# Filter groups in twos, rows of the last groups from two queues, and a projection moved ahead: a four-layer kernel on one core

## Chip, cores and metric

One core of a Trainium2 chip runs the whole kernel. Its engines are TensorE (PE, with its weight loads as PEld), VectorE (DVE), ScalarE (ACT), GpSimd (POOL) and SyncE (SP); each runs its own instructions in the order in which they were written. The metric is the device time of one execution in microseconds (us), lower is better.

## What is computed

The input x has 2048 rows and 576 columns, in float32. Two layers are applied in turn, each twice (`_layernorm` has no weights):

```python
def _A_ref(x, wqkv, wo):          # H = 32 heads of 18, window W = 256
    q, k, v = split((x @ wqkv))
    scores = einsum("bhqd,bhkd->bhqk", q, k) * Dh ** -0.5
    scores = where((i - j >= 0) & (i - j < W), scores, -1e9)
    return (softmax(scores) @ v) @ wo

def _B_ref(x, w_r, w_i):
    X = rfft2(x) * (w_r + 1j * w_i)
    return irfft2(X, s=(S, D))

x = x + _A_ref(_layernorm(x), A_wqkv, A_wo)
x = x + _B_ref(_layernorm(x), B_w_r, B_w_i)
x = x + _A_ref(_layernorm(x), A_wqkv, A_wo)
x = x + _B_ref(_layernorm(x), B_w_r, B_w_i)
```

## The kernel before

The 2048 rows are 16 tiles of 128 (NT = 16). The program runs `layer_a`, `layer_b`, `layer_a`, `layer_b`, each overlapping its neighbours at the borders. Everything is written out by hand: an instruction stands in its engine's queue where the Python code emits it. `pipe(n, [(lag, fn), ...])` calls, at step s, each `fn` for tile s − lag, in the order of the list. A DMA is issued by the engine whose queue it is written in; those of SP and ScalarE share eight semaphore lanes in rotation, and one waits until the last transfer on its lane has landed. DMAs of GpSimd have lanes of their own.

**layer_a.** `first_tiles` writes the beginning of the first one by hand, before the steps of a loop with lags go on: `ld` loads a tile, `sq`, `bn`, `bn2` make mean and variance, `f0` normalises (`axn`), `f1` transposes it on PE (`tpaa`, `tpba`) and splits it in high and low parts `xh`, `xl` on ScalarE and VectorE, `f2` multiplies by the weights of v (`vps`) and copies the result (`vt`) for a store to `v_d`. Then `proj` makes q and k by quarters of 512 rows: PE `pj`, ScalarE copies to `sg`, VectorE the remainder, a DMA stores it to `qk_d`, from where it is loaded into `qs` and `ks`. A tiny activation `ex` (L1045) is written ahead of them so that the table of exponentials is loaded early; its one-element tile comes from the pool `wp` of that stage. `score_max` finds row maxima; `m_rows` (L1134) turns the negated maxima of a quarter (`mt`) into rows of `qs` by four small DMAs (L1144); `exps` makes E on PE and P = exp(E) on ScalarE. For the first two quarters of the first head group the four DMAs are ScalarE's, later SP's.

**layer_b.** The output projection of layer_a (`out.unit`, PE tile `ops`, 28 matmuls for a tile of rows, then two VectorE additions in `late`) is interleaved with the forward transform: in the second layer `norm(u)` is the norm of tile u (`out.stats`, then `fy`), `out.sums` its squares on ScalarE, `back(n)` is `f3` (PE `pz`) and `f4` (copy `half`, sums `ye`, DMA issues). `f4` stores `ye` to DRAM as `yd[0]`, and for tiles from 11 on copies eight rows directly into the tiles of the first two filter groups. In the second layer the stores of tiles 12 and 13 are held until tile 15 and then issued by ScalarE.

The filter stage runs over 16 groups g. `g0` loads y, `gw` the weights, `g1m` makes `p2_g` on PE (eight matmuls of 128 rows into 64 columns; the page's counts of eight include the halves), four products on VectorE (L475, L476 with two tiles each) and `uv` on GpSimd; `g2` makes `pq` on PE (L488), a copy `both` on ScalarE (L510), a difference on GpSimd (L513) and two on VectorE (L514, L515), and stores the result (`ze`, or `eo` for even groups) as `yd[1]`. PSUM comes from `Banks`: tiles with the tag "mm" rotate over three slots.

```python
zs, held = {}, []
pipe(16, [(10, g2), (7, g1m), (2, gw), (0, g0)])
```

The inverse stage follows, `pipe` over the 16 tiles with `ly` (load a tile, L545), `i1` (PE `pi`), `i2` (transposes) and `i3` (PE `po`, and the output). The first `near` tiles (2 in the first layer_b, 3 in the second) aren't loaded by `ly`: `g2` puts them together in SBUF, the groups below FG = 11 by `older` reads from `yd[1]` (L519), the others by `rows`, a DMA of eight rows from SBUF to SBUF (L495):

```python
def rows(eng, n2, k):
    eng.dma_start(yis[n2][8 * k:8 * k + 8]..., zs[k][8 * n2:8 * n2 + 8])
```

The store of group 13 is held and issued after the rows of group 15. Between the stages of the second layer_b `warm(n)` runs n matmuls whose result nobody uses. In the first layer_b five further tiles (`w0`, `w1`, `w2`, PE `wo`) of layer weights run beside the stages; `w1(3)` (transposes, and the ScalarE copy `et19`) follows the copy of group 15.

Of the kernel before, what the change touches and what calls it, by code (L numbers as in the profile page):

```python
# [117 lines left out]
class Banks:  # L118
# [6 lines left out]
    def tile(self, shape, dtype, tag, name, bufs):  # L125
        if tag != "mm":
            return self.pools[tag not in self.lower].tile(shape, dtype, tag=tag, name=name, bufs=bufs)
        self.turn = (self.turn + 1) % 3
        return self.pools[self.turn == 2].tile(shape, dtype, tag=tag, name=name, bufs=2 if self.turn < 2 else 1)

def layer_b(tc, xf, dst, dcs, gc, ident, rh, rl, out, ga_d, fc_d, m2_d, w_d, wo_d, wo2_d, dram, nxt, share):
# [8 lines left out]
    FD, FG, SH = 11, 11, 192  # L140
    near, NY = (2, 3) if first else (3, 4)
    with ExitStack() as stack:
# [152 lines left out]
        def f4(n2, h):  # L295
            pz = h["pz"]
            ye = wp.tile([128, 2, NF], F32, tag="ye", name=f"ye{n2}", bufs=NY)
            if not first and NT - 4 <= n2 < NT - 1:
                if "both" not in h:
                    f4c(n2, h)  # L300
                both = h["both"]
                V.tensor_add(ye[:, 0], pz[:, 0, 0:NF], both[:, 1])
                P.tensor_sub(ye[:, 1], both[:, 0], both[:, 1])
            else:
                both = ip.tile([128, 2, NF], F32, tag="both", name=f"half{n2}", bufs=2)
                A.copy(both[:, 0], pz[:, 1, 0:NF])
# [103 lines left out]
        else:  # L410
# [51 lines left out]
        def g1m(g, h):  # L462
            ps = pp.tile([128, 2, 512], F32, tag="mm", name=f"p2_{g}", bufs=3)
# [17 lines left out]
        def g2(g, h):  # L481
            pq = pp.tile([128, 2, 512], F32, tag="mm", name=f"pq{g}", bufs=3)
# [14 lines left out]
            if g == 15:  # L497
# [3 lines left out]
                if first:  # L501
                    w1(3)
                else:
                    rows(nc.scalar, 2, 13)
                    rows(nc.scalar, 2, 14)
                for n2 in range(near):
                    rows(nc.sync, n2, 15)
                held.pop()()
            else:
                A.copy(both, pq[:, :, 0:NF])  # L510
                if near > 2 and g in (FG + 1, FG + 2):
                    rows(nc.scalar, 2, g - 1)
# [3 lines left out]
            if g in (FG - 1, FG + 1):  # L516
                lo, hi = (0, 8) if g < FG else (8, FG)
                for n2 in range(near):
                    nc.sync.dma_start(yis[n2][8 * lo:8 * hi].rearrange("p c f -> p (c f)"), yd[1][n2, lo:hi].rearrange("g i f -> (g i) f"))  # L519
# [6 lines left out]
            if g == 13:  # L526
                held.append(store)
            else:
                store()
# [135 lines left out]
class Out:  # L665
# [108 lines left out]
    def late(self, u):  # L774
        oL = self.oL[u % 3]
        h, l = oL[:, 0:128], oL[:, 128:256]
        self.steps(u, [(h, "h", 3), (l, "h", 3), (h, "l", 3)], False, True)
        x = self.xt(u)
# [29 lines left out]
    def unit(self, u, pp):  # L808
        ps = pp.tile([128, 2, 512], F32, tag="mm", name=f"ops{u}", bufs=3)
        self.early(u, [ps[:, 0], ps[:, 1]])  # L810
        self.late(u)
# [11 lines left out]
def layer_a(tc, ident, eps, bp, src, dst, wqk_d, wv_d, wo_d, dc_d, gc_d, dram, copy, wvs, second, spectral, share):  # L823
# [17 lines left out]
    if True:  # L841
# [24 lines left out]
        with tc.tile_pool(name="a1", bufs=2) as wp, ExitStack() as banks:  # L866
# [108 lines left out]
            def first_tiles():  # L975
# [32 lines left out]
                f2(0, h[0], slice(1, 14))  # L1008
                f2(1, h[1], slice(0, 8))
# [4 lines left out]
            for s in range(0 if second else 7, NT + 7 + late):  # L1014
# [7 lines left out]
                for lag, fn in ((0, ld), (6 + late, f1), (4, sq), (4 + second, bn2), (4 + 2 * second, f0), (3, bn), (7 + late, f2)):  # L1022
                    if 0 <= s - lag < NT:
# [7 lines left out]
        with ExitStack() as c2:  # L1031
# [13 lines left out]
            A.activation(wp.tile([128, 1], F32, name="ex", bufs=1), eps, AF.Exp)  # L1045
# [88 lines left out]
            def m_rows(n, c):  # L1134
# [5 lines left out]
                for hp in range(2):  # L1140
                    for pair in range(2):
                        r = (hp * 2 + pair) * 4
                        b = 64 * hp + 63
                        (nc.sync if n or c > 1 else nc.scalar).dma_start(q[b:b + 1, pair, c * 512:c * 512 + 512].rearrange("a (t q) -> a t q", t=4).bitcast(F32),  # L1144
# [328 lines left out]
```

## Time and profile before

| | us |
|---|---|
| median of three runs (1383.33, 1384.60, 1388.88) | 1384.6 |
| the profiled execution | 1387.57 |
| its span, first to last instruction | 1385.1 |
| PE busy | 1343.1 (97%) |
| VectorE, ScalarE, GpSimd busy | 893.3, 785.4, 640.0 |
| TensorE clock granted, mean | 0.994 |
| filter stage, first layer_b (p of group 0 to pq of group 15) | 605.1 to 643.4 |
| filter stage, second layer_b | 1269.7 to 1312.1 |

In the rows of the profile an instruction is named by its line in the kernel (L488), engine, operation, and output and input tiles without their numbers (`pq<-uv,m`); "x8" means eight in a row. `ofree` is a large shared buffer in which y, the tiles `yis` and x lie. ACTq, SPq are the DMA issues of an engine's queue, times in us from the start of the span. In brackets stands the idle time ahead of a row and what ended it.

### The profile page before, as it was taken

The page shows a single profiled execution, that of the slowest core. Times are in us where ns is not written, and L with a number is a line of the kernel's source. Part 1 is how long each engine was busy: PE and PEld are TensorE (multiplying, and loading weights), DVE is VectorE, ACT ScalarE, POOL GpSimd, SP SyncE. Part 2 cuts the span into 40 slices and gives each one's busy share as a digit, 9 for nine tenths or more (in the row PEclk, how much of TensorE's full clock was granted, in tenths as well). Part 3 has the DMA queues.
Part 4 walks back from the last instruction along what each step waited for, and adds up shares of the span by engine and source line. Part 5 has one row for each costly group of instructions (what it writes and reads, how often), then busy time and mean ns, then how long its engine had stood idle before and what let it go on. Part 6 is the DMA issues. An engine that isn't in the chain of part 4 may idle for free.

```text
span 1385.1 us, 33553 instructions
## 1 busy us (share of the span) xinstructions
PE 1343.1 (97%) x11356; PEld 1001.1 (72%) x11356; DVE 893.3 (64%) x3046; ACT 785.4 (57%) x1978; POOL 640.0 (46%) x1140
## 2 busy tenths in 40 slices
PE   8999999999999999998999999999999999998988
PEld 8986666666665699975999866666666655897577
DVE  4417777877778266666673157787777883564745
ACT  5522777777778544443355316777777777563223
POOL 2257555555447443475221394554545457102711
PEclk9999999999999999999999999999999999999999
DMA  6756655655446457678763468555555465597864
GB/s 192 211 160 204 190 181 174 189 167 163 145 150 185 109 166 239 218 244 258 254 224 73 107 199 232 169 163 168 165 157 143 151 181 147 171 349 247 257 224 158
DMA packets 202159, 259.09 MB, mean 187 GB/s; under 512 B 104270, under 2 KB 109646, under 8 KB 201478
## 3 DMA queue, kind: packets, MB, share of 16 engines
q1 hardware_dynamic: 191494, 235.63, 55.8%
q10 hardware_dynamic: 8000, 15.63, 3.2%
q0 software_dynamic: 2496, 5.71, 1.5%
q8 instruction: 91, 1.49, 0.4%
q14 instruction: 78, 0.64, 0.2%
HBM read 156.26 MB, written 101.01 MB: 186 GB/s over the span
## 4 chain that ended last, share of the span: by engine, by line
PE 83%; DMA 5%; ACT 3%; DVE 3%; POOL 2%; issue 2%; SPq 1%; ACTq 0%; DVEq 0%; POOLq 0%
PE pj L1067 16%; PE S L1124 12%; PE U L1181 11%; PE vps L963 8%; PE ops L758 7%; PE E L1161 5%; PE po L251 4%; PE pq L488 2%; PE pf L251 2%; PE p L467 2%; PE tpo L1195 2%; PE pi L551 2%; ACT P L1162 2%; PE pz L289 2%; DMA yd<-ze 1%
## 5 line engine op out<-in xcount | busy, mean ns | idle before, releaser
L1126 DVE CUSTOM_DVE_ANT_0 jk<-S,mask 128x384 bf16<-128x384 f32 (+2 forms) x1024 | 490.4, 529 | 109.4 <-PE E L1161 56.1
L1162 ACT ACTIVATE P<-E 128x384 f32<-128x384 f32 (+2 forms) x1024 | 409.0, 476 | 121.9 <-PE E L1161 98.7
L1164 POOL TENSOR_SCALAR_AFFINE_SELECT P<-P 128x512 f32<-128x512 f32 x256 | 163.1, 637 | 277.9 <-ACT P L1162 254.3
L1124 PE MATMUL S<-ks,qs 63*128 63x384 f32 (+2 forms) x1024 | 269.1, 371 | 1.0 <-DVE m L1126 0.4
L1161 PE MATMUL E<-qs,ks 64*128 64x384 f32 (+2 forms) x1024 | 222.2, 372 | 3.3 <-ACT P L1162 2.6
L1124 PEld LDWEIGHTS S<-ks,qs 63*128 63x128 f32 x1024 | 140.7, 185 | 105.2 <-DVE m L1126 73.1
L1181 PE MATMUL U<-P,vq 128*19 128x128 f32 (+1 forms) x3840 | 187.8, 328 | 1.0 <-ACT us L1186 1.0
L1067 PE MATMUL pj<-xh,wqh 128*128 128x512 f32 x360 | 156.4, 434 | 3.3 <-DVE sg L1082 2.8
L1181 PEld LDWEIGHTS U<-P,vq 128*19 128x19 f32 x3840 | 95.7, 98 | 77.5 <-issue 21.7
L1167 POOL TENSOR_SCALAR_AFFINE_SELECT P<-P 128x512 f32<-128x512 f32 x224 | 142.8, 638 | 0.0
L1161 PEld LDWEIGHTS E<-qs,ks 64*128 64x128 f32 x1024 | 114.1, 185 | 17.0 <-ACT P L1162 8.2
L1067 PE MATMUL pj<-xh,wql 128*128 128x512 f32 x360 | 124.5, 419 | 0.5 <-POOL wql L648 0.5
L1067 PE MATMUL pj<-xl,wqh 128*128 128x512 f32 x288 | 122.1, 424 | 0.0
L758 PE MATMUL ops<-oroom 128*128 128x290 f32 (+1 forms) x812 | 116.3, 300 | 0.2
L758 PEld LDWEIGHTS ops<-oroom 128*128 128x128 f32 x812 | 111.4, 191 | 0.7 <-DVE ofree L781 0.7
L1067 PEld LDWEIGHTS pj<-xh,wqh 128*128 128x128 f32 x360 | 67.9, 189 | 34.8 <-issue 10.8
L1082 DVE TENSOR_TENSOR sg<-pj,sg 128x512 fp32r<-128x512 f32 x72 | 49.5, 687 | 58.3 <-ACT sg L1079 58.3
L1126 DVE DVE_READ_ACCUMULATOR2_ANT m<- 128x1 f32 x1024 | 85.2, 83 | 0.0
L1067 PEld LDWEIGHTS pj<-xh,wql 128*128 128x128 f32 x360 | 64.2, 189 | 20.9 <-issue 10.6
L1079 ACT CAST sg<-pj 128x512 fp32r<-128x512 f32 x72 | 42.2, 586 | 61.8 <-PE pj L1067 44.9
L243 ACT CAST et<-tp 128x512 fp32r<-128x512 f32 x53 | 31.2, 588 | 77.8 <-PE tp L239 76.7
L963 PE MATMUL vps<-wvh,xh 128*128 128x288 f32 x320 | 70.6, 302 | 0.2
(224 smaller groups left out, 2303.6 us busy)
## 6 DMA issues: line engine op xcount, KB each, us to landing
qk_d<-sg SPq DMA_DIRECT2D x56, 512.0 KB
qs<-qk_d SPq DMA_DIRECT2D x384, 72.0 KB
ks<-qk_d SPq DMA_DIRECT2D x348, 72.0 KB
v_d<-vt SPq DMA_DIRECT2D x32, 304.0 KB
vq<-v_d SPq DMA_DIRECT2D x16, 608.0 KB
wt<-in_w SPq DMA_DIRECT2D x16, 580.0 KB
ofree<-x SPq DMA_DIRECT2D x16, 580.0 KB
x<-ofree SPq DMA_DIRECT2D x32, 290.0 KB
```

The source lines that it names most:

```text
L251: T.matmul(ps[:, c, 0:NF], tail[r] if si == 4 else hl_(si), dcs[b // 2][r, b % 2], start=mi == si == 0, stop=si == 4)
L758: self.nc.tensor.matmul(self.ps[u][n][:, 0:self.n], x, self.w[p][:, (2 * wk + n) * self.n:(2 * wk + n + 1) * self.n], start=first and i == ...
L963: T.matmul(ps[:, n, 0:288], xT(xk, c), w[:, wk, n * 288:(n + 1) * 288], start=i == 0, stop=i == len(ks) - 1)
L1067: T.matmul(box["ps"].rearrange("r (n p) -> r n p", n=NT) if second else box["ps"], w[:, wk], x, start=s == 0, stop=s == len(ks) - 1)
L1082: V.tensor_sub(rest[:, 1], by, rest[:, 0].bitcast(F32))
L1124: T.matmul(ps[:, 0:N], q[b:b + 63, pair, i * 128:i * 128 + 128], k[b:b + 63, pair, lo:hi], start=True, stop=True)
L1126: V.tensor_tensor_reduce(out=jk[:, 0:N], in0=ps[:, 0:N], in1=mask[:, 384 - N:384], scale=1.0, scalar=-3e38, op0=ALU.add, op1=ALU.max, accu ...
L1161: T.matmul(ps[:, 0:nq], k[b:b + 64, pair, j * 128:j * 128 + 128], q[b:b + 64, pair, j * 128:j * 128 + nq], start=True, stop=True)
L1162: A.activation(p[:, hl_, 0:nq], ps[:, 0:nq], AF.Exp, scale=SC)
L1164: P.affine_select(out=p[:, :, 0:128], in_=p[:, :, 0:128], pattern=[[0, 4], [1, 128]], compare_op=ALU.is_ge, fill=0.0, base=0, channel_mult ...
L1167: P.affine_select(out=p[:, :, 256:384], in_=p[:, :, 256:384], pattern=[[0, 4], [-1, 128]], compare_op=ALU.is_gt, fill=0.0, base=0, channel ...
L1181: T.matmul(U[32 * h:32 * h + 19, (q0 % 4) * 128:(q0 % 4) * 128 + 128 * (q1 - q0)], vts[n][:, j, h], pt[n, j][:, h, (q0 - j) * 128:(q1 - j) ...
```

## The change

Five things are changed.

1. In `first_tiles` the statistics and the norm of tile 3 are written ahead of the last part of tile 1's v product, before the step of the loop in which they stood.
2. The filter stage takes the groups in twos: p of two groups, then pq of two groups. PSUM slots are named: p uses the two buffers of one slot in turn, pq of odd groups the third "mm" buffer, pq of even groups the "tp" buffer, and groups 14 and 15 the buffers of p. The stores of both groups follow both. FG is 12 and `near` is 3 in both layers. Rows of groups 12 to 15 for tiles 0 and 1 are issued by SP, those for tile 2 by GpSimd after each odd group. The reads of groups 8 to 11 are issued by ScalarE, after group 15's copy and ahead of `w1(3)`. `warm(36)` becomes `warm(40)`.
3. In the second layer_b the 28 matmuls of the last output projection stand ahead of `back(11)`, its additions where they stood before; the held stores of tiles 12 and 13 follow the rows and the store of tile 15 in the code.
4. The maxima rows of the second quarter are issued by SP instead of ScalarE.
5. The tile `ex` comes from another pool.

The core of the diff (`both_` calls `g1m` for two groups at odd steps):

```diff
         self.turn = (self.turn + 1) % 3
-        return self.pools[self.turn == 2].tile(shape, dtype, tag=tag, name=name, bufs=2 if self.turn < 2 else 1)
+        return self.slot(self.turn, name)
+
+    def slot(self, k, name):
+        self.turn = min(k, 2)
+        return self.pools[k > 1].tile([128, 2, 512], F32, tag="tp" if k == 3 else "mm", name=name, bufs=2 if k < 2 else 1)
...
-    FD, FG, SH = 11, 11, 192
-    near, NY = (2, 3) if first else (3, 4)
+    FD, FG, SH, near = 11, 12, 192, 3
+    NY = 3 if first else 4
...
                 A.copy(both[:, 0], pz[:, 1, 0:NF])
-                if not first and n2 == NT - 1:
-                    for k in (n2 - 3, n2 - 2):
-                        hs[k]["store"](nc.scalar)
...
                 h["store"] = store
+            if not first and n2 == NT - 1:
+                for k in (n2 - 3, n2 - 2):
+                    hs[k]["store"](nc.scalar)
...
+                if u == b - 1:
+                    out.unit(b, pp, False)
                 back(u - 3)
                 out.sums(u)
                 norm(u)
-            out.unit(b, pp)
+            out.add(b)
...
-            ps = pp.tile([128, 2, 512], F32, tag="mm", name=f"p2_{g}", bufs=3)
+            ps = pp.slot(g % 2, f"p2_{g}")
...
-            pq = pp.tile([128, 2, 512], F32, tag="mm", name=f"pq{g}", bufs=3)
+            pq = pp.slot(3 - g % 2 if g < 14 else g - 14, f"pq{g}")
...
-                if first:
-                    w1(3)
-                else:
-                    rows(nc.scalar, 2, 13)
-                    rows(nc.scalar, 2, 14)
-                for n2 in range(near):
-                    rows(nc.sync, n2, 15)
-                held.pop()()
...
-                if near > 2 and g in (FG + 1, FG + 2):
-                    rows(nc.scalar, 2, g - 1)
...
-            if g in (FG - 1, FG + 1):
-                lo, hi = (0, 8) if g < FG else (8, FG)
+
+            def older(eng, lo, hi):
                 for n2 in range(near):
...
-            if FG <= g < 15:
+            if g == 10:
+                older(nc.sync, 0, 8)
+            if g >= FG:
                 for n2 in range(2):
-                    rows(P if g == 14 and n2 else nc.sync, n2, g)
+                    rows(nc.sync, n2, g)
+                if g % 2:
+                    for k in (g - 1, g):
+                        rows(P, 2, k)
+            if g == 15:
+                older(nc.scalar, 8, FG)
+                if first:
+                    w1(3)
+                held.pop()()
...
-        zs, held = {}, []
-        pipe(16, [(10, g2), (7, g1m), (2, gw), (0, g0)])
+        def pair(g, h):
+            if g % 2:
+                for k in (g - 1, g):
+                    g2(k, filt[k])
+                while stores:
+                    stores.pop(0)()
...
+        pipe(16, [(7, both_(g1m)), (9, pair), (2, one(gw)), (0, one(g0))])
...
-            warm(36)
+            warm(40)
...
                 bn(3, h[3])
                 f2(0, h[0], slice(1, 14))
+                sq(3, h[3])
+                bn2(3, h[3])
+                f0(3, h[3])
                 f2(1, h[1], slice(0, 8))
...
-            A.activation(wp.tile([128, 1], F32, name="ex", bufs=1), eps, AF.Exp)
+            A.activation(bp.tile([128, 1], F32, tag="ex", name="ex", bufs=1), eps, AF.Exp)
...
-                        (nc.sync if n or c > 1 else nc.scalar).dma_start(q[b:b + 1, pair, c * 512:c * 512 + 512].rearrange("a (t q) -> a t q", t=4).bitcast(F32),
+                        (nc.sync if n or c else nc.scalar).dma_start(q[b:b + 1, pair, c * 512:c * 512 + 512].rearrange("a (t q) -> a t q", t=4).bitcast(F32),
```

PE's queue in the second filter stage, before (`p2_g` is p of group g):

```order
L467 MATMUL p2_2_19889<-ofree_17769,fc_18884 64x290 x4
L488 MATMUL pq0_19900<-uv0_19874,m2_18885 128x290 x4
L467 MATMUL p2_3_19911<-ofree_17769,fc_18884 64x290 x4
L488 MATMUL pq1_19923<-uv1_19885,m2_18885 128x290 x4
L467 MATMUL p2_4_19935<-ofree_17769,fc_18884 64x290 x4
L488 MATMUL pq2_19946<-uv2_19897,m2_18885 128x290 x4
L467 MATMUL p2_5_19957<-ofree_17769,fc_18884 64x290 x4
L488 MATMUL pq3_19969<-uv3_19919,m2_18885 128x290 x4
```

And the same place after:

```order
L473 MATMUL p2_2_19892<-ofree_17772,fc_18887 64x290 x4
L473 MATMUL p2_3_19903<-ofree_17772,fc_18887 64x290 x4
L494 MATMUL pq0_19914<-uv0_19877,m2_18888 128x290 x4
L494 MATMUL pq1_19924<-uv1_19888,m2_18888 128x290 x4
L473 MATMUL p2_4_19938<-ofree_17772,fc_18887 64x290 x4
L473 MATMUL p2_5_19949<-ofree_17772,fc_18887 64x290 x4
L494 MATMUL pq2_19960<-uv2_19900,m2_18888 128x290 x4
L494 MATMUL pq3_19970<-uv3_19911,m2_18888 128x290 x4
```

PE went from one kind to the other at every group and now does so at every second one; p of groups 4 and 5 stands between pq of groups 1 and 2, and pq of group 0 follows p of group 3.

PE's queue in the second layer_b where the last output projection stood, before:

```order
L758 MATMUL ops14_19667<-oroom_17768 128x290 x28
L289 MATMUL pz11_19699<-yh2_18894,oroom_17768 128x290 x4
L289 MATMUL pz11_19699<-yl2_18897,oroom_17768 128x290 x2
L758 MATMUL ops15_19724<-oroom_17768 128x290 x28
L289 MATMUL pz12_19756<-yh0_18892,oroom_17768 128x290 x4
```

And after:

```order
L775 MATMUL ops14_19670<-oroom_17771 128x290 x28
L775 MATMUL ops15_19702<-oroom_17771 128x290 x28
L293 MATMUL pz11_19731<-yh2_18897,oroom_17771 128x290 x4
L293 MATMUL pz11_19731<-yl2_18900,oroom_17771 128x290 x2
L293 MATMUL pz12_19759<-yh0_18895,oroom_17771 128x290 x4
```

The six matmuls of pz11 moved behind the 28 of tile 15.

SP's queue at the end of the second filter stage, before (`eo2`, `ze13`, `eo3`, `ze15` are the results of groups 12 to 15, `x2` the next rows of x):

```order
L495 DMA ofree_17769<-ze11_20164 8x580 x2
L525 DMA yd1_18868<-ze11_20164 16x8x580
L519 DMA ofree_17769<-yd1_18868 24x580 x3
L495 DMA ofree_17769<-eo2_18888 8x580 x2
L495 DMA ofree_17769<-ze13_20217 8x580 x2
L495 DMA ofree_17769<-eo3_18889 8x580
L495 DMA ofree_17769<-ze15_20244 8x580 x3
L525 DMA yd1_18868<-ze13_20217 16x8x580
L525 DMA yd1_18868<-ze15_20244 16x8x580
L164 DMA ofree_17769<-x2_61 128x1160 x2
L545 DMA ofree_17769<-yd1_18868 128x580 x2
```

And after:

```order
L532 DMA yd1_18871<-ze11_20166 16x8x580
L501 DMA ofree_17772<-eo2_18891 8x580 x2
L501 DMA ofree_17772<-ze13_20213 8x580 x2
L501 DMA ofree_17772<-eo3_18892 8x580 x2
L501 DMA ofree_17772<-ze15_20241 8x580 x2
L532 DMA yd1_18871<-ze13_20213 16x8x580
L532 DMA yd1_18871<-ze15_20241 16x8x580
L168 DMA ofree_17772<-x2_61 128x1160 x2
L562 DMA ofree_17772<-yd1_18871 128x580 x2
```

The three reads of groups 8 to 10 and the rows of group 11 have left SP's queue; the rows of tile 2 are no longer in it, and those of group 14 are both in it.

More of the change, by code (lines that the diff above doesn't have):

```diff
@@ L515, in g2 @@
                 V.tensor_sub(ye[:, 1, SH:NF], pq[:, 0, SH:NF], both[:, 1, SH:NF])
-            if g in (FG - 1, FG + 1):
-                lo, hi = (0, 8) if g < FG else (8, FG)
+            def older(eng, lo, hi):
                 for n2 in range(near):
-                    nc.sync.dma_start(yis[n2][8 * lo:8 * hi].rearrange("p c f -> p (c f)"), yd[1][n2, lo:hi].rearrange("g i f -> (g i) f"))
-            if FG <= g < 15:
+                    eng.dma_start(yis[n2][8 * lo:8 * hi].rearrange("p c f -> p (c f)"), yd[1][n2, lo:hi].rearrange("g i f -> (g i) f"))
+            if g == 10:
+                older(nc.sync, 0, 8)
+            if g >= FG:
                 for n2 in range(2):
-                    rows(P if g == 14 and n2 else nc.sync, n2, g)
+                    rows(nc.sync, n2, g)
[7 more added lines that the diff above has]
+                held.pop()()
             def store():
@@ L528, in g2 @@
             else:
-                store()
-        zs, held = {}, []
-        pipe(16, [(10, g2), (7, g1m), (2, gw), (0, g0)])
+                stores.append(store)
+        def pair(g, h):
[4 more added lines that the diff above has]
+                    stores.pop(0)()
+        zs, held, stores = {}, [], []
+        both_ = lambda fn: lambda g, h: [fn(k, filt[k]) for k in (g - 1, g)] if g % 2 else None
+        filt = [dict() for _ in range(16)]
+        one = lambda fn: lambda g, h: fn(g, filt[g])
+        pipe(16, [(7, both_(g1m)), (9, pair), (2, one(gw)), (0, one(g0))])
         if first:
@@ L772, in early, with late @@
         self.steps(u, ks[some], some.start == 0, False)
-    def late(self, u):
+    def late(self, u, add=True):
         oL = self.oL[u % 3]
@@ L777, in late, with add @@
         self.steps(u, [(h, "h", 3), (l, "h", 3), (h, "l", 3)], False, True)
+        if add:
+            self.add(u)
+    def add(self, u):
         x = self.xt(u)
@@ L806, in stats, with unit @@
         V.reciprocal(rs, rs)
-    def unit(self, u, pp):
+    def unit(self, u, pp, add=True):
         ps = pp.tile([128, 2, 512], F32, tag="mm", name=f"ops{u}", bufs=3)
         self.early(u, [ps[:, 0], ps[:, 1]])
-        self.late(u)
+        self.late(u, add)
     def ahead(self, u, pp, loads=True):
@@ L1022, in layer_a @@
                 for lag, fn in ((0, ld), (6 + late, f1), (4, sq), (4 + second, bn2), (4 + 2 * second, f0), (3, bn), (7 + late, f2)):
-                    if 0 <= s - lag < NT:
+                    if 0 <= s - lag < NT and (second or (s, lag) != (7, 4)):
                         fn(s - lag, hold[s - lag], *([slice(8, 14)] if s == 7 and lag == 6 and not second else []))
```

## The prediction

> **What bounds the kernel now.** I began with the page's busy times, followed the chain of waits, and then looked at the stretches in which TensorE (PE) waits.
>
> ```profile
> PE 1343.1 (97%) x11356; PEld 1001.1 (72%) x11356; DVE 893.3 (64%) x3046; ACT 785.4 (57%) x1978; POOL 640.0 (46%) x1140
> ```
>
> PE is the bound: 1385.1 − 1343.1 leaves 42 us of the span in which it does nothing. A change can shorten the kernel in three ways: less PE time for the same matmuls, fewer waits of PE, or fewer matmuls at a lowered clock. This one tries the first in the filter stage and the others at the stage borders. Here is the chain in the first layer_b, from the filter stage to the inverse stage (start, length, what, count).
>
> ```profile
> 607.31 1.95 PE p L467 x16
> ...
> 611.42 1.13 PE p L467 x8
> 612.54 1.18 PE pq L488 x8
> ...
> 640.23 2.18 PE pq L488 x16
> ...
> 649.30 3.82 DMA yd<-ze
> 653.26 3.83 DMA ofree<-yd
> ```
>
> Inside the stage the chain is PE alone, 2.31 us for each group; behind it the last store and the read that follows it set the time. These are PE's rows at that border (the bracket is the idle time ahead and what ended it):
>
> ```profile
> 644.91 1.61 PE L251 MATMUL wo<-dc,et 128*128 128x290 f32 x10 [0.68 <-ACT et L243]
> ...
> 649.47 2.20 PE L551 MATMUL pi<-ofree,ga 128*128 128x290 f32 x8 [1.75 <-DMA ofree<-ze]
> ...
> 657.22 2.22 PE L551 MATMUL pi<-ofree,ga 128*128 128x290 f32 x4 [3.02 <-DMA ofree<-yd]
> ...
> 662.48 1.14 PE L551 MATMUL pi<-ofree,ga 128*128 128x290 f32 x4
> ```
>
> After 3.02 us without work the same four matmuls take 2.22 us instead of 1.14: PE's clock was lowered. The second layer_b, PE's rows again, from the last output projections to the first inverse tiles:
>
> ```profile
> 1254.74 3.81 PE L758 MATMUL ops<-oroom 128*128 128x290 f32 x27
> ...
> 1269.66 0.71 PE L467 MATMUL p<-ofree,fc 128*64 128x290 f32 x4 [2.16 <-DMA ofree<-ye]
> ...
> 1275.36 2.20 PE L467 MATMUL p<-ofree,fc 128*64 128x290 f32 x8 [2.53 <-DMA ofree<-yd]
> 1277.50 2.70 PE L488 MATMUL pq<-uv,m 128*128 128x290 f32 x8
> ...
> 1312.14 5.08 PE L333 MATMUL warm<-dc 128*128 128x290 f32 x36
> 1319.57 3.82 PE L551 MATMUL pi<-ofree,ga 128*128 128x290 f32 x8 [2.35 <-DMA ofree<-eo]
> ...
> 1325.78 0.33 PE L236 MATMUL tp<-ident,ofree 128*128 128x128 f32 x1 [0.75 <-DVE et L245]
> ...
> 1329.79 1.25 PE L551 MATMUL pi<-ofree,ga 128*128 128x290 f32 x4 [1.25 <-DMA ofree<-yd]
> ```
>
> Gaps of 2.35 and 2.53 us were followed by slow matmuls, those of 2.16 and 1.75 were not; I put the border between 2.2 and 2.3 us. The chain through the same stretch shows what those gaps wait for:
>
> ```profile
> 1262.42 0.55 PE pz L289 x2
> ...
> 1269.26 3.10 DMA yd<-ye
> 1272.44 2.79 DMA ofree<-yd
> ...
> 1308.77 5.59 DMA yd<-ze
> ...
> 1318.60 0.62 SPq L495
> ...
> 1319.27 0.59 SPq L525
> ...
> 1319.90 3.97 DMA yd<-ze
> 1323.95 5.79 DMA ofree<-yd
> ```
>
> **Filter groups in twos (both layers).** In the trace a group alone costs 1.13 (p) + 1.18 (pq), so two cost 4.62 us. Sixteen p matmuls in a row take 1.95, eight therefore 0.98, and each entry into p from pq costs 1.13 − 0.98 = 0.15. Two pq in a row take 2.18 with their entry. A pair is then 0.15 + 1.95 + 2.18 = 4.28, which is 0.34 less, seven times: 2.4 us in each layer. It holds only if nothing else needs more than 4.28 per pair. The first stage as a window (busy time of PE, weight loads, VectorE, ScalarE and GpSimd, then clock, DMA share and GB/s), and the groups of rows of the other engines in the middle of the second:
>
> ```profile
> 611.00:640.00 29.00, 29.00 (x202) 14.59 (x200) 24.13 (x50) 8.36 (x13) 23.15 (x38) 1.00 0.90 306
> ```
>
> ```profile
> L475 DVE TENSOR_TENSOR ofree<-p,wt 128x580 f32<-128x580 f32 x12 | 9.0, 752 | 0.0
> L478 POOL TENSOR_TENSOR uv<-ofree 128x290 f32<-128x290 f32 x12 | 8.4, 700 | 5.9 <-DVE ofree L475 5.9
> L510 ACT COPY both<-pq 128x580 f32<-128x580 f32 x13 | 8.4, 643 | 36.8 <-PE pq L488 36.8
> L514 DVE TENSOR_TENSOR ze<-pq,both 128x290 f32<-128x290 f32 x6 | 2.8, 460 | 2.1 <-ACT both L510 2.1
> ```
>
> Of 4.62 us VectorE is busy 24.13/29.00, which is 3.84 per pair, and GpSimd 23.15/29.00, 3.69. Both stay under 4.28, VectorE by 0.4 only. The order helps: p of the next pair stands ahead of this pair's pq, so uv has about 2.1 us of other PE work to arrive in, and the slots of pq, freed by the sums, lie idle over the next pair's p. The transfers are the tighter thing. In the first layer the DMA engines are busy for 0.90 of the stage at 306 GB/s. With 2.4 us less, the same bytes ask for 0.98, and the even groups' two eo buffers must be stored within four groups' time, now 8.6 instead of 9.2 us, with the even store held back for its pair. So I take 1.5 of the 2.4 us there (ends 0 and 2.4) and the full 2.4 in the second layer, whose eo buffers are four (ends 1.2 and 2.4).
>
> **End of the first filter stage.** `near` goes from 2 to 3, so pi2 no longer waits for the store and the read back: 3.02 us, and 2.22 − 1.14 = 1.08 for its cold matmuls, and by the same ratio about 0.5 (an estimate) for the transposes behind: some 4.6. The rows of groups 12 to 15 for two tiles, 0.6 each, are the only ones left between SP and pi0 and pi1, and the read of groups 8 to 11 leaves SP's queue; of the 1.75 ahead of pi0 I count 0.7 as gone. Against it, three reads now stand on ScalarE ahead of the copy that makes et for wo; they wait until the stores of groups 10 and 11 have landed, issued some 7 us before the last pq ends (two pairs of 4.28, less 1.4 for copy and sums; landing takes 3.8 to 5.6 us by the rows above), and take about 0.6 each to issue. That is up to 1.8 more ahead of the 644.91 row, which today waits 0.68. What is late next is pi3, whose read waits for stores 13 and 15; with 3.8 + 3.8 us behind an issue 4 us after the last pq, it is there before PE has done pi0 to pi2. Ends −1.8 and −5.3; I take the middle, −3.5.
>
> **Start of the second filter stage.** The last output projection (28 matmuls, 3.81 us) now precedes pz11, so pz11, half11 and everything behind them on ScalarE and VectorE (the squares, the norm of tile 15, pz15, ye15) come about 3.8 us later. What pays for it: in the trace the rows of tile 15 and its store wait on SP for lanes held by the stores of tiles 12 and 13, and that last store starts only at 1269.26. After the change these two stores stand behind it. Tile 15's pz ended at 1262.97; with about 1.4 for the copy and the sums, its result was there at 1264.4, so now 1268.2; two rows of 0.62 go out and the store starts by 1269.5, and it lands near 1272.6 instead of 1272.36. The stores of tiles 12 and 13, issued at about 1268 on ScalarE, land 3.1 to 5.5 us later, and the read for p2 must wait for them too: 0.2 to 1.1 us of delay. On the other side, p0 and p1 come about 1.1 later, so the gap ahead of p2 shrinks from 2.53 to between 1.5 and 2.5, and if it stays under 2.2, p2 and pq0 run at full speed: 2.20 − 1.13 and 2.70 − 1.18, together some 2.5 us. Delay 0.6 against half of 2.5: I take −0.5, ends +1.1 and −2.2.
>
> **End of the second filter stage.** SP no longer waits for the store that takes 5.59 and then three reads; it has four rows of tiles 14 and 15 behind the last pq, then the stores of 13 and 15. Last pq ends at 1312.14 = E. The sum of group 15 is ready near E + 1.5; two rows to E + 3.0, two stores to E + 4.3, landing 3.97, read 5.79: pi3 at E + 14.1 instead of E + 17.65 (1329.79). Before it PE has warm(40) (40/36 of 5.08: 5.6), pi0 to pi2, three sets of transposes and two of po: 8.2 us between 1319.57 and 1329.79 without their two waits, 6.4 without the cold start (3.82 against 2.0), so until E + 12. The gap ahead of pi3 is thus about 2.1 us, at the border of cooling; if it cools, 1.7 come back. Ends −1.8 and −3.5; I take −2.5.
>
> The Trainium skill, "TensorE: Matmul & The Clock Gate", section "What's actually happening", gives an idle window of about 3.4 us, free-running, before the clock is halved. By that rule none of these gaps would lower the clock, and the term would be −3.5; the trace shows it after 2.35 us, and I go by the trace. The skill's "DMA: Bandwidth & Descriptors", "Anatomy of one DMA", gives about 2.0 us plus bytes at 436 GB/s: an estimate of 2.7 us for the read of 0.3 MB, against 5.79 in the row. By the page pi3 would be ready 3.1 us sooner and the gap would be gone.
>
> **The edits in layer_a.** First the tiles at the start, then the maxima, PE's rows and ScalarE's:
>
> ```profile
> 18.70 0.87 ACT L929 ACTIVATE axn<-ax,nb,rs 128x576 f32<-128x576 f32 x1 [0.66 <-DVE nb L925]
> 19.62 0.66 PE L659 MATMUL tpaa<-ident,axn 128*128 128x128 f32 x4 [0.87 <-ACT axn L929]
> ```
>
> ```profile
> 129.12 3.01 ACTq L1144 DMA_DIRECT2D qs<-mt x4
> 133.20 0.44 PE L1161 MATMUL E<-qs,ks 64*128 64x384 f32 x1 [1.59 <-ACT P L1162]
> 837.03 0.44 PE L1161 MATMUL E<-qs,ks 64*128 64x384 f32 x1 [1.01 <-ACT P L1162]
> ```
>
> ```profile
> 87.09 0.50 PE L1067 MATMUL pj<-xh,wqh 128*128 128x512 f32 x1 [1.42 <-DVE sg L1082]
> 787.58 1.28 ACT L1045 ACT_TABLE_LOAD   x1 [3.63 <-DMA v_d<-vt]
> 790.39 0.51 PE L1067 MATMUL pj<-xh,wqh 128*128 128x512 f32 x1 [0.60 <-DVE sg L1082]
> ```
>
> The norm of tile 3 now stands ahead of ScalarE's casts for tile 2, so the 0.87 go: −0.9 (ends 0 and −0.9). The four maxima rows (3.01 us of ScalarE's queue ahead of the cast and the exponentials) leave for SP: PE's 1.59 and 1.01 go, −2.6 (ends −1.0 and −2.6). SP pays those issues; queued behind them are a store of qk_d and later loads, which nothing needs for tens of microseconds. The table load no longer waits for the stores of v; but the copy to sg behind it does now. In the second layer I count 0.4 of the 0.60; in the first, GpSimd's zeroing of q and k follows next, so I count nothing there (ends 0 and 1.4 for the two).
>
> **The sum.** −1.5 − 2.4 − 3.5 − 0.5 − 2.5 − 0.9 − 2.6 − 0.4 = −14.3 us. The profiled execution took 1387.6 us (span 1385.1), which gives 1373.3. It is 3.0 above the median 1384.6 of the three runs, so against the median the forecast is 1370.3 us.
>
> **The rivals.**
> (1) *The borders don't pay.* Waits move instead of going: wo waits 1.8 more for et, the clock falls ahead of pi3 and p2. For it: two of my gaps lie within 0.3 us of the cooling border, and SP still issues its rows one after another. Against it: pi2's 3.02 us goes whatever the rest does. The three border terms fall from −6.5 to between −1 and +1; 1384.6 − 7.8 = 1376.8, within a range of 1375 to 1380.
> (2) *The transfers are the bound.* The pair's period stays at 4.62 because stores of eo land too late (5.59 us in the row above, against about 7 available) or the DMA engines are full. For it: the 0.90. Against it: PE has no gap in the 29 us of that row, so reads keep ahead of it today. The switches then give nothing: 1384.6 − 10.4 = 1374.2.
> (3) *The pairs run one step after another, and it gets slower.* If a slot is held until the previous pair's sums are done, p must wait for them. The serial loop is 2.10 (p), 0.75 (last product), 0.70 (uv), 2.18 (pq), 0.64 (copy), 0.7 (a long and a short sum): 7.1 us at the least, 2.5 more than now, in 14 pairs: +35, less the other 10.4, makes 1409. It decides from 4.62 + 10.4/14 = 5.36 us per pair. For it: VectorE's products of one pair stand behind the sums of the last, with only some 0.5 us free in a period. Against it: the slots alternate between p and pq, and the order lets p run ahead.
> (4) *A part does not do what it says*: SP could be so late with the maxima that the first E of the next quarter waits for them; that costs back at most the 2.6 gained and stays inside the range.
>
> **How the numbers follow.** About 0.5% (6.9 us) is what a measurement here can tell from no change, so faster means under 1377.7 us. Forecast 0.64, of which all is faster; borders 0.16, of which half is faster; transfers 0.12, all faster; serial 0.08, slower. That gives 0.84 faster, 0.08 same; the single profile makes each term uncertain, so I move 0.03 to same: 0.81, 0.11, 0.08. The favourable ends sum to −20.7 (1363.9), the unfavourable to −4.7 (1379.9), which is also where the first rival ends; the range is 1364 to 1380, and only the serial case and a little of the first rival lie outside.
>
> **What would show it.** Right: p x16 and pq x16 alternating in PE's rows every 4.28 us without gaps; no gap ahead of pi2 in the first layer; pi3 near E + 14 in the second; store of tile 15 issued near 1269.5 on the old time scale; no idle time ahead of E at 133 and 837. Wrong: gaps released by uv or by the sums inside the filter stage, p rows over 2.2 us each, wo waiting over 2 us for et, or pi3 still 17 us after the last pq.

## The result

The change made the kernel slower: 1397.4 us (median of six runs, 1396.2 to 1400.8) against 1382.4 us before (six runs, 1379.0 to 1388.9), a ratio of 1.0108 with the interval 1.0082 to 1.0134. The forecast was 1370.3 us. The profiled execution after has a span of 1394.6 us, 9.5 more than the one shown of before, which was itself 5 us above the median of its six runs.

The page's busy times after (lines of the changed kernel lie some 4 to 24 above those of before):

```profile
PE 1344.6 (96%) x11360; PEld 1007.8 (72%) x11360; DVE 892.8 (64%) x3046; ACT 786.8 (56%) x1978; POOL 641.7 (46%) x1146
```

PE is busy 1.5 us longer than before, although the filter stage gained; it waits some 8 us more. Where, PE's rows show. First the two layer_a, at the quarter whose maxima rows moved to SP:

```profile
141.46 0.66 PE L1185 MATMUL E<-qs,ks 64*128 64x384 f32 x1 [3.92 <-DMA qs<-mt]
...
851.98 0.66 PE L1185 MATMUL E<-qs,ks 64*128 64x384 f32 x1 [5.98 <-DMA qs<-mt]
```

Two waits for the rows that did not exist before, and 0.66 for a matmul that took 0.44: the granted clock was 0.50 behind both (141.4 to 144.0 and 851.9 to 853.5). Next the first layer_b, filter stage and its end:

```profile
614.60 2.54 PE L473 MATMUL p<-ofree,fc 128*64 128x290 f32 x16 [0.59 <-PE p L473]
617.06 3.40 PE L494 MATMUL pq<-uv,m 128*128 128x290 f32 x16
620.39 2.17 PE L473 MATMUL p<-ofree,fc 128*64 128x290 f32 x16
622.50 2.23 PE L494 MATMUL pq<-uv,m 64*128 64x290 f32 x16
624.66 2.17 PE L473 MATMUL p<-ofree,fc 128*64 128x290 f32 x16
...
653.89 2.78 PE L255 MATMUL wo<-dc,et 128*128 128x290 f32 x10 [5.09 <-ACT et L247]
...
663.04 1.15 PE L568 MATMUL pi<-ofree,ga 128*128 128x290 f32 x4
```

From 620.39 to 624.66 a pair takes 4.27 us, as forecast, and pi2 no longer waits; but wo waits 5.09 where it waited 0.68. The second layer_b:

```profile
1275.25 0.79 PE L293 MATMUL pz<-yh,oroom 128*128 128x290 f32 x4 [3.90 <-DVE ofree L802]
...
1289.72 2.17 PE L473 MATMUL p<-ofree,fc 128*64 128x290 f32 x16 [1.22 <-DVE ofree L481]
...
1330.38 3.88 PE L568 MATMUL pi<-ofree,ga 128*128 128x290 f32 x8 [2.08 <-DMA ofree<-ze]
...
1339.29 1.14 PE L568 MATMUL pi<-ofree,ga 128*128 128x290 f32 x4
```

The start of the same instruction in the two traces, after minus before, along the program:

| place in before (us) | offset (us) |
|---|---|
| tile 3's transposes, 19.62 | −1.0 |
| first proj, 87.09 | −2.5 |
| S, first layer_a, 111.5 | +0.2 |
| E, 181.8 | +6.2 |
| p of group 0, first layer_b, 605.1 | +5.7 |
| last pq, first layer_b (its end, 643.4) | +4.6 |
| pi4, 666.0 | +5.0 |
| pj, second layer_a, 790.4 | +4.1 |
| S, 885.2 | +14.1 |
| ops of tile 14, second layer_b, 1250.0 | +12.0 |
| p of group 0, 1269.7 | +15.7 |
| last pq (its end, 1312.1) | +10.6 |
| pi3, 1329.8 | +9.5 |

Between 111 and 182 the program loses 6.0 us and between 837 and 885 another 10 (3.9 to 14.1). Both lie at the maxima rows. This is what SP did there after, and before:

```profile
126.06 0.85 SPq L1131 DMA_DIRECT2D vq<-v_d  x1
127.00 1.29 SPq L874 DMA_DIRECT2D wqr<-in_wqk  x1
128.35 3.35 SPq L1123 DMA_DIRECT2D qs<-qk_d  x6
133.97 1.97 SPq L1108 DMA_DIRECT2D qk_d<-sg  x2
136.04 2.85 SPq L1168 DMA_DIRECT2D qs<-mt  x4
```

```profile
126.91 1.36 SPq L1084 DMA_DIRECT2D qk_d<-sg  x2
132.30 0.34 SPq L1107 DMA_DIRECT2D vq<-v_d  x1
132.73 0.38 SPq L853 DMA_DIRECT2D wqr<-in_wqk  x1
133.16 3.42 SPq L1099 DMA_DIRECT2D qs<-qk_d  x6
```

After, the rows go out at 136.04, behind the load of v, a weight, six loads of q for the next head group and two stores. Before, ScalarE issued them at 129.12, ahead of the load of v at 132.30. The shared semaphore lanes decide that order. Here is what SP waited for between 118 and 145, before and after (what waits, for what, us in total, times, longest):

```profile
SPq L1107 <- DMA qs<-mt: 4.0, 1, 4.0
```

```profile
SPq L1108 <- DMA vq<-v_d: 2.2, 1, 2.2
SPq L1108 <- DMA wqr<-in_wqk: 1.1, 1, 1.1
```

Before, a lane that one of the rows held kept back the load of v. After, v and the weight went first, and the two stores written ahead of the rows waited until these had landed. In the second layer_a the same two waits are 1.3 and 1.7 us.

### The profile page after: what moved, and what is told of

The parts are those of the page before. It is cut to its first block, busy times and chain, and to the rows that moved or that the text cites. A ratio compares the mean times of both kernels' runs of the same rounds, so it can differ in the third digit from the quotient of the medians.

```text
span 1394.6 us, 33585 instructions
## 1 busy us (share of the span) xinstructions
PE 1344.6 (96%) x11360; PEld 1007.8 (72%) x11360; DVE 892.8 (64%) x3046; ACT 786.8 (56%) x1978; POOL 641.7 (46%) x1146
## 4 chain that ended last, share of the span: by engine, by line
PE 82%; DMA 5%; ACT 3%; DVE 3%; POOL 3%; issue 3%; SPq 1%; ACTq 0%; DVEq 0%; POOLq 0%
PE pj L1091 16%; PE S L1148 12%; PE U L1205 11%; PE vps L984 8%; PE ops L775 7%; PE E L1185 5%; PE po L255 4%; PE pf L255 2%; PE pi L568 2%; PE tpo L1219 2%; PE p L473 2%; ACT P L1186 2%; PE pq L494 2%; PE pz L293 2%; DMA qs<-mt 1%
## 5 line engine op out<-in xcount | busy, mean ns | idle before, releaser
L1091 PE MATMUL pj<-xh,wql 128*128 128x512 f32 x360 | 127.9, 429 | 2.3 <-POOL wql L665 2.3
```

Source lines behind the costliest of these rows:

```text
L1091: T.matmul(box["ps"].rearrange("r (n p) -> r n p", n=NT) if second else box["ps"], w[:, wk], x, start=s == 0, stop=s == len(ks) - 1)
```

## The experiments

Each ratio is to the time of the kernel before that was measured beside the run: 1383.3 us for experiments 1 to 4, 1382.3 for 5 to 8 and 1383.4 for 9 to 12.

**1. The maxima rows from ScalarE again** (on the changed kernel).

```diff
-(nc.sync if n or c else nc.scalar).dma_start(q[b:b + 1, ...
+(nc.sync if n or c > 1 else nc.scalar).dma_start(q[b:b + 1, ...
```

> The changed kernel with the maxima rows of the second quarter issued by ScalarE again. Theory Q (queue): on SP they stand behind a v load, a weight load, six q loads and two stores, and E waits for them; both traces of the pair of kernels show the offset growing by 6.2 us in the first layer_a and 9.9 us in the second at this place, so 16 us come back: 1381 us (1378 to 1384), and no wait of E for the rows above 2 us. Rival B (borders): the loss lies in the filter stages and their borders, and the offsets in layer_a are shifts that a later wait would swallow anyway: 1394 to 1397 us.

1379.5 us (ratio 0.9970, 0.9958 to 0.9983). Its rows of E at the two places:

```profile
130.51 0.44 PE L1185 MATMUL E<-qs,ks 64*128 64x384 f32 x1 [1.05 <-ACT P L1186]
...
832.37 0.44 PE L1185 MATMUL E<-qs,ks 64*128 64x384 f32 x1 [1.00 <-ACT P L1186]
```

The queue theory holds: this one line is the whole loss and more. The other edits together gain, but 4 us, not 12.

**2. The kernel before with that line alone.**

```diff
-(nc.sync if n or c > 1 else nc.scalar).dma_start(q[b:b + 1, ...
+(nc.sync if n or c else nc.scalar).dma_start(q[b:b + 1, ...
```

> The kernel before with this one edit, the maxima rows of the second quarter from SP. Theory Q: 1382.4 + 16 = 1398 us (1394 to 1401). Rival B: what the prediction said of this edit, 1382.4 - 2.6 = 1380 us.

1397.0 us (1.0101, 1.0082 to 1.0119), within the theory's range. The waits:

```profile
141.84 0.65 PE L1161 MATMUL E<-qs,ks 64*128 64x384 f32 x1 [5.13 <-DMA qs<-mt]
...
851.71 0.65 PE L1161 MATMUL E<-qs,ks 64*128 64x384 f32 x1 [4.24 <-DMA qs<-mt]
```

**3. The rows on SP, the next head group's loads behind them** (on the changed kernel).

```diff
-                if t in (-4, 4, 8, 12):
+                if t in (-1, 4, 8, 12):
                     stack_load(1, max(t, 0) // 4)
```

> The changed kernel, maxima rows on SP, but the first loads of q and k for the next head group are written three steps later, behind them. Theory Q: what stands ahead makes the delay, so the waits of E for the rows (3.9 and 6.0 us) fall under 1.5 us and the time to 1381 to 1386 us. Rival T (transfers): the rows are slow because SP's small transfers are slow there; the waits stay over 3 us and the time at 1394 to 1398 us.

1387.6 us (1.0032, 1.0019 to 1.0045), between the two theories. The trace is of one of its slowest executions (1392.1 us). SP's queue, then E:

```profile
126.76 1.01 SPq L1131 DMA_DIRECT2D vq<-v_d  x1
127.86 1.23 SPq L874 DMA_DIRECT2D wqr<-in_wqk  x1
129.18 1.21 SPq L1108 DMA_DIRECT2D qk_d<-sg  x2
130.49 3.97 SPq L1168 DMA_DIRECT2D qs<-mt  x4
134.50 4.70 SPq L1123 DMA_DIRECT2D qs<-qk_d  x6
```

```profile
138.56 0.41 PE L1185 MATMUL E<-qs,ks 64*128 64x384 f32 x1 [1.29 <-DMA qs<-mt]
...
847.18 0.66 PE L1185 MATMUL E<-qs,ks 64*128 64x384 f32 x1 [4.51 <-DMA qs<-mt]
```

The issue is 5.5 us earlier than in the changed kernel (130.49), but E still starts only at 138.56. By the times, the loads that stood ahead are about half of the loss (9.8 of the 17.9 us between the changed kernel and the first experiment). Rows of 2 KB then needed 5.4 to 7.9 us to land, with the load of v and two stores ahead of them.

**9. The load of v behind them as well** (on the third).

```diff
-                if t + LEAD == 5:
+                if t + LEAD == 9:
                     v_load(0)
```

> The third experiment with the load of v (0.6 MB) written behind the maxima rows too. In the third the rows were issued 5 to 9 us earlier than in the changed kernel but landed only 5.4 to 7.9 us after their issue, each right behind the transfer that SP had issued before it. Theory O (SP's transfers land in their order, so a row waits for the big ones ahead of it): without v's 0.6 MB the rows land about 2.5 to 3 us sooner, E's wait in the second layer_a falls from 4.5 us to under 2.5, that of the first from 1.3 to under 0.7, and the time from 1387.6 to 1383 to 1385.5 us. Rival G (the transfers of the other queues slow them): the rows land 5 to 8 us after their issue as before, 1387 to 1388 us.

1384.8 us (1.0012, 0.9998 to 1.0026). No E waits for the rows any more; the values do instead:

```profile
141.25 0.97 PE L1205 MATMUL U<-P,vq 128*19 128x256 f32 x5 [2.00 <-DMA vq<-v_d]
...
846.56 0.62 PE L1205 MATMUL U<-P,vq 128*19 128x256 f32 x7 [1.41 <-DMA vq<-v_d]
```

In the first layer_a the rows landed some 4 us sooner than in the third, 2.5 of them because they were issued sooner (127.97), and still 5 to 7.4 us after their issue in the two layers. The waits of E went further down than theory O said, and the time came out where it put it; but how long the rows are under way hardly fell, as G said. What the third and this one show is that loads written behind the rows let them out sooner and shorten E's waits. Why the rows stay so long under way is open. ScalarE's rows went on another DMA queue than SP's transfers (q10 and q1 in the profile) and landed 1.7 to 3.2 us after their issue in the kernel before, against 2.8 to 5.3 from SP in the changed kernel. That speaks for the order on SP's own path; but while ScalarE's rows went, SP's loads stood back, so a lighter load on the DMA engines as a whole is not ruled out.

**4. The copies for wo ahead of ScalarE's reads** (on the changed kernel).

```diff
-                older(nc.scalar, 8, FG)
                 if first:
                     w1(3)
+                older(nc.scalar, 8, FG)
```

> The changed kernel, in the first layer_b with the transposes and copies for wo written ahead of ScalarE's three reads of groups 8 to 11. If those reads hold up the copy, the wait of 5.1 us ahead of wo falls to about 0.7 us, the slow clock behind it goes, and the time falls by 3 to 6 us, to 1392 to 1395 us. Rival: the next wait, of the first inverse tile for the same reads, takes its place, and the time stays at 1396 to 1398 us.

1395.3 us (1.0086, 1.0070 to 1.0102), just outside the first range, and the interval overlaps that of the changed kernel. The wait moved:

```profile
648.61 1.34 PE L255 MATMUL wo<-dc,et 128*128 128x290 f32 x8 [0.68 <-ACT et L247]
...
654.88 2.65 PE L568 MATMUL pi<-ofree,ga 128*128 128x290 f32 x5 [2.65 <-DMA ofree<-ze]
```

In the changed kernel ScalarE stood in front of those reads until the store of group 11, issued by SP at 643.41, had landed:

```profile
650.15 3.07 ACTq L515 DMA_DIRECT2D ofree<-yd  x3
653.26 0.59 ACT L247 CAST et<-tp 128x512 fp32r<-128x512 f32 x1 [4.50 <-DMA ofree<-yd]
```

With the copies ahead wo runs on time, and pi0 waits for the rows instead. Some 2 us of the 5 are left by the medians, which the intervals don't tell from none.

**5. The projection behind pz11 again** (on the first).

```diff
-                if u == b - 1:
-                    out.unit(b, pp, False)
                 back(u - 3)
...
-            out.add(b)
+            out.unit(b, pp)
```

> The kernel of the first experiment (changed, maxima rows from ScalarE), with the last output projection behind pz11 again. Theory C: the projection ahead holds the chain of tile 15 and, through its PSUM slot, pz13 (wait of 3.9 us); in that kernel the offset against the kernel before goes from -5.0 us at pz11 to -1.2 at p of group 0 and is back at only -1.8 at p of group 2, so 1.5 to 3 us come back: 1376.5 to 1378 us against 1379.5, and the wait of 3.9 us is gone. Rival R: the read that p of group 2 waits for decides, and the time stays at 1379 to 1380 us.

1377.1 us (0.9965, 0.9953 to 0.9977). That is in the range of theory C, but the kernel before was 1 us faster beside this group; the ratio is 0.0005 (0.7 us) below the first's, and the intervals overlap. The wait of 3.90 is gone, and another has grown:

```profile
1258.59 0.81 PE L293 MATMUL pz<-yh,oroom 128*128 128x290 f32 x4 [0.60 <-ACT yh L285]
...
1267.38 0.72 PE L471 MATMUL p<-ofree,fc 128*64 128x290 f32 x4 [2.75 <-DMA ofree<-ye]
1267.89 0.69 PE L473 MATMUL p<-ofree,fc 128*64 128x290 f32 x4
1268.38 0.99 PE L471 MATMUL p<-ofree,fc 128*64 128x290 f32 x4
1269.05 1.28 PE L473 MATMUL p<-ofree,fc 128*64 128x290 f32 x4
```

p of group 0 now starts 20.3 us after ops of tile 14 instead of 23.5 and runs into a lowered clock; the last pq ends 58.8 us after those ops, in the first experiment 61.6, before 62.2, in the changed kernel 60.7. This pair of traces gives the projection's place 2.8 us, but two further kernels with the same second stage (experiments 11 and 12) have 57.2 and 60.3. That the wait of 3.90 came from the projection is shown; what its place costs in time is not.

**6. Free slots for the first two p** (on the first).

```diff
-            ps = pp.slot(g % 2, f"p2_{g}")
+            ps = pp.slot(g % 2 if g > 1 else 3 - g, f"p2_{g}")
```

> The kernel of the first experiment, with p of groups 0 and 1 in the two slots that pq does not yet use. Theory S: p of groups 2 and 3 waits for the products of groups 0 and 1 because p now has two buffers; a wait of 0.6 and one of 1.9 us at that place and the same again where two rows are taken as one. It falls to what the read of y leaves, the time by 1 to 2.5 us to 1377 to 1378.5. Rival R: the reads take the place of the slot, and the time stays within 0.5 us of 1379.5.

1378.5 us (0.9973, 0.9961 to 0.9985): in time not told from the first. The traces show the slot wait all the same. The start of the second filter stage, in the first experiment and here:

```profile
1273.55 2.17 PE L473 MATMUL p<-ofree,fc 128*64 128x290 f32 x16 [1.87 <-DVE p L482]
```

```profile
1272.36 2.25 PE L473 MATMUL p<-ofree,fc 128*64 128x290 f32 x16 [0.86 <-DMA ofree<-yd]
```

VectorE's products no longer hold p of group 2; the read of y does, 1.0 us sooner counted from p of group 0 (1268.50 and 1268.32). In the first layer_b the stage takes 36.3 us from there to the last pq instead of 37.2. So theory S is right on the wait. In the second layer_b the pi behind give it back: pi3 comes 16.3 us after the last pq, in the first experiment 15.0.

**7. Reads of groups 8 and 9 alone, copies first** (on the first): the diff of the fourth, and

```diff
-    FD, FG, SH, near = 11, 12, 192, 3
+    FD, FG, SH, near = 11, 10, 192, 3
```

> The kernel of the first experiment, in the first layer_b wo's copies ahead of ScalarE's three reads, and those reads for groups 8 and 9 alone (FG 10), so that they need stores that are one pair older. Theory L (the landing of the stores of 10 and 11 holds the reads, and pi0 behind them): the wait of 4.1 us ahead of wo goes to about 0.7, that of pi0 stays under 1.5, time 1375 to 1377 us. Rival I (issue): four more rows on SP take 2.6 us and pi0 waits as long as it does with the copies alone moved (2.65 us): 1378 to 1379.5 us.

1380.9 us (0.9989, 0.9977 to 1.0001): a miss for both. In the first layer_b a lane now held ScalarE (wo waited 3.0 us). FG also holds for the second layer_b, where more rows delayed pi0:

```profile
1314.35 4.21 PE L568 MATMUL pi<-ofree,ga 128*128 128x290 f32 x8 [3.58 <-DMA ofree<-ze]
```

**8. The edits of 5, 6 and 7 together.**

> All three edits on the kernel of the first experiment. If they act at separate places, their gains add: 1379.5 - 2 - 1.7 - 3.5 = 1372.3 us (1370.5 to 1375). Rival R: they meet the same reads, and the time is no lower than the best of the three alone, about 1376.

1378.2 us (0.9965, 0.9949 to 0.9982). The gains don't add (1372.3 was expected for that), and the time is no lower than the best of the three, as rival R said. p of group 0 came 19.6 us after ops of tile 14 (23.5 in the first), then the read and the rows took most of it back:

```profile
1269.44 3.17 PE L471 MATMUL p<-ofree,fc 128*64 128x290 f32 x12 [2.78 <-DMA ofree<-yd]
...
1313.77 1.79 PE L566 MATMUL pi<-ofree,ga 128*128 128x290 f32 x3 [4.24 <-DMA ofree<-ze]
```

**10. The two edits of layer_a alone** (on the kernel before: tile 3's norm, and `ex` in the other pool, as in the diff of the change).

> The kernel before with the two small edits of layer_a alone, tile 3's norm sooner and the tile of the table load from the other pool. The trace of the first experiment has the offset against before at -3.5 us when the first filter stage begins. If that is the edits' doing, 1382.7 - 3.5 - 0.5 (the second table load) = 1378.7 us (1377.5 to 1380). Rival: the prediction's 0.9 + 0.4, 1381.4 us.

1381.1 us (0.9986, 0.9969 to 1.0002), unclear in the time and nearest to the rival. In its trace tile 3's transposes start 1.1 us sooner and the first proj behind the table load 2.8, of which 1.2 go again into the wait for GpSimd's weights.

**11. The filter stages alone** (the fifth without those two edits).

> The fifth experiment without those two edits of layer_a: the kernel before with the groups in twos, their rows, reads and stores, the stores of tiles 12 and 13 behind tile 15, and nothing else. If the parts add, 1377.1 + 4.0 = 1381 us (1380 to 1382), so 1.5 us less than before. By the prediction's terms for this part (1.5 + 2.4 + 3.5 + 2.5) 1373 us.

1379.3 us (0.9973, 0.9959 to 0.9987), so 4.1 us less than before, two fifths of what the prediction's terms for this part came to (9.9), and just under the range that was expected if the parts add. This and the tenth together come to 6.5 us, the fifth, which has both, to 5.2; the intervals allow for the difference.

**12. The fifth with the copies for wo first**, the diff of the fourth.

> The fifth experiment with wo's copies ahead of ScalarE's reads in the first layer_b. In the fourth the same edit took about 2 us off the changed kernel, though pi0 then waited 2.65 us; here 1377.1 - 2 = 1375 us (1374 to 1376.5), the lowest of all. Rival: within 0.7 us of 1377.1, as the wait of pi0 replaces that of wo.

1376.1 us (0.9950, 0.9934 to 0.9967), the lowest here, in the expected range and faster than both kernels: 7 us under before and 21 under the changed one. Its gain over the fifth is within the intervals.

## Why the prediction was wrong

**The maxima rows** decide it. The step that failed is the sentence that SP pays the issues and what is queued behind them is needed by nobody. It asked who stands behind the rows, not what stands ahead: on SP they came 6.9 us later (136.04 instead of 129.12), behind stores that waited for 0.6 MB of v and a weight to land, and in the second layer_a 14.1 later (847.55 instead of 833.46), of which 3.9 is the offset there. The term was −2.6 us; in the traces of the two kernels it was +16, alone on the kernel before +14 by time. The first rows of the quarter are needed at once: E of key tile 2 covers query tiles 2 to 4, and tile 4 is in that quarter. The fourth rival named this wait and said it could cost at most the 2.6 gained; nothing bounded it so.

**Groups in twos**: the period of 4.28 is 4.27, and neither the transfers nor VectorE broke it. The first pair was forgotten: with two buffers, p of groups 2 and 3 waits for the products of 0 and 1 (experiment 6). From p of group 0 to the last pq the first stage gained 1.1 us in the trace (1.5 forecast), and the same in all traces of the changed stage but those of experiments 6 and 8, which take the free slots.

**End of the first stage**: the step "up to 1.8 more" for the reads ahead of et was mis-sized; wo waited 5.09, 4.4 more. The store of group 11 was issued 4.6 us before the last pq ended (643.41), not 7, because the pq of the last two pairs stand directly behind one another; put at 3.8 to 5.6 us, it landed 6.7 us later, when ScalarE could go on at 650.15. The second read then waited again, until 652.32. The term was −3.5 and came out +0.4 (offsets 4.6 at the last pq and 5.0 at pi4). With the copies first, the rows of pi0 replace the wait: the rival of waits that move was right here; with them pi4 comes 21.9 us after the last pq in the fourth experiment and 20.5 in the twelfth, before 22.6.

**Start of the second stage**: the chain's delay was foreseen, but not that the projection's PSUM slot is one of three and is freed by additions that stand behind tile 14's norm, so that pz13 waits 3.90. p of group 0 came 3.7 us later (offset 12.0 to 15.7), not 1.1. From ops of tile 14 to the last pq the gain is 1.4 us where the two terms together had 2.9. Traces differ by as much here: 60.6 to 62.3 us with the second stage of before (before, experiments 2 and 10), 60.3 to 61.6 with that of the change (after, 1, 3, 4 and 9), 57.2 to 60.3 without the projection (5, 11 and 12). Of pq of group 0 (2.70) only 0.5 us was the clock: in the kernel before the first layer_b takes 2.22 for it, at 609.19, without any gap.

**End of the second stage**: pi3 came 16.6 us after the last pq instead of 14.1 (1339.29 − 1322.69). pi0 was the late one, 7.7 us after instead of 5.6, and the clock fell behind its wait. SP had eight rows to issue there, from 1321.94 to 1328.14, where the prediction counted four; a wait for a lane is 0.5 us of that. In the first experiment pi3 comes 15.0 after, a gain of 2.6 against before, and −2.5 was forecast. That agreement is partly luck: the traces with the old order (before, 2 and 10) have 15.8 to 17.6, those with the new order and FG 12 have 15.0 to 16.6. The estimate of 2.7 us for pi3's read, from the Trainium skill, "DMA: Bandwidth & Descriptors", "Anatomy of one DMA", uses a fit that the section gives for GpSimd's path; SP issued this read, and it took 4.4 us in the changed kernel (from 1333.30).

**First tiles and table load**: 1.0, a little past its end, and, in the second layer, about 0.8 in the trace. In the first layer the table load gained another 1.4 at the first proj, but by 111.5 all of it was lost again at the wait for GpSimd's weights and the lowered clock behind it (offsets −2.5 and +0.2). In the trace of the first experiment the clock held there, and 2.2 of 3.3 us stay.

Without the maxima rows the forecast would have been −11.7 and the measurement is −4 (experiment 1): the direction of the rest was right, its size three times too large. Experiments 4, 5 and 6 show it at the borders: a removed wait was mostly replaced by one that had been hidden behind it.

## What to carry to other kernels

Before moving a transfer to another queue, list what stands ahead of it there at that moment, how many bytes these carry, how long they take to land and which of their semaphore lanes it shares, and find the first reader of what is moved; its price has no upper bound in the wait it removes. A DMA wait in front of an engine's next copy costs the landing time of the store it reads, so put the copy first, and ask which wait is hidden just behind the one removed. A change that rotates fewer buffers pays at the first round, when nothing has yet come free.

## What the runs showed of the hardware

The idle time after which PE's clock falls has no fixed border. In the changed kernel 2.08 us ahead of pi0 were followed by 3.88 us for its eight matmuls (row above), and 1.84 us at 108.90 by 2.07 us for four that took 1.20 before; in the twelfth experiment 2.25 us were not followed by a slow stretch:

```profile
1310.30 2.19 PE L566 MATMUL pi<-ofree,ga 128*128 128x290 f32 x8 [2.25 <-DMA ofree<-ze]
```

In the fifth experiment the clock fell only after PE had begun again (0.72 and 0.69, then 0.99 and 1.28 for equal work). In the changed kernel's trace each stretch at clock 0.50 lasts 3.41 us or a multiple of it, the last one of the program aside (3.41 from 1330.60, 6.83 from 139.35, 10.24 from 849.32). A gap can thus cost up to 1.7 us on top of itself (an estimate, half of 3.41). The Trainium skill, "TensorE: Matmul & The Clock Gate", section "What's actually happening", says that the window which decides is free-running; that agrees with a border that moves, while its length there, about 3.4 us of idleness, is more than these gaps.
